# Decode layer on one core: the K part of pair 31 ahead of the output projection, the last O_l built on POOL, the residual joined in PSUM, the last rows of W_down in two transfers

## Chip, cores, metric

One core of a Trainium2 chip runs the whole kernel. The metric is the device time of one execution in microseconds (us). Times within a profile count from the start of its span. The device time is 1.2 to 1.4 us longer than the span of the profile in most runs.

PE is the matmul engine; DVE, ACT and POOL are the vector, scalar and GpSimd engines; SP issues most of the DMA transfers. SBUF is the on-chip memory that the engines read, PSUM the one that PE writes its products to. A transfer is spread over up to 16 DMA engines and has landed when the last of them has raised its semaphore. The granted clock is the share of full speed that the profile records for PE. Scatter means highest less lowest time.

## The reference, cut to what matters

```python
B, Sq, D = 2, 1, 512
Hq, Hkv, Sk, Dh = 32, 32, 8192, 128
F = 1376
h  = x + Attention(layernorm(x), k_cache, v_cache, wq, wo)      # 32 heads, 8192 cached positions
h2 = h + (relu(ln(h) @ W_gate) * (ln(h) @ W_up)) @ W_down       # W_down has 1376 rows = 10 * 128 + 96
```

K and V caches are 268 MB in bf16, and everything is read once. A "pair" is two heads of one batch row; there are 32, numbered 0 to 31, each with 4 MB of K and 4 MB of V.

## The kernel before: the parts that matter

Each engine has its own program, joined by semaphores. For one pair, DVE multiplies K by q for 96 of the 128 positions that each partition holds (one operation of 6.56 us, line 540), folds the product in four adds (line 549) and reduces it; PE transposes and multiplies the other 32 (`k_part`) and does P·V (`pv`). The last two pairs, P0 = 30 and P1 = 31, stand outside the loop. There, the heads done so far must pass through the output projection. For that, the scaled head output `O_cur` is spread into `O_l`, PE gathers it (`o_gather`), ACT copies it to `O_all`, and PE multiplies it with `X` (the rows of wo).

```python
def o_spread(g, prog, *t_oc):                 # five small operations; e is DVE or POOL
    e = prog.eng
    prog.wait(tok("og", g), *t_oc)
    ... prog.run(e.memset(O_l[...], 0.0)); prog.last()
    for a in range(2):
        e.tensor_copy(out=rsel[:, a, :], in_=rows[...])
        i = e.tensor_tensor(out=O_l[:, a, :, p0:p0 + n], in0=O_cur[...], in1=mask[...], op=ALU.mult)
    i.then_inc(l2p, 1)

# PE, after the loop (cut)
k_part(tail, P0, (2, 3, 4, 5), ((k2p, 1),))
nc.tensor.wait_ge(l2p, 1)
o_gather(tail)
...                                           # projection with X, 30 matmuls; then W product from os_sb
k_part(tail, P1, (10, 11, 12, 13), ((k2p, 2),))
pv(tail, P0, ...)
pv(tail, P1, ...)

# DVE, pair 30 (cut); the multiply of pair 31 comes behind it
normalize(Ob, dve.run, dve.last)
o_spread(g - 1, dve, dve.run(o_scale()))

# SP: the FFN weights; then at the very end of the stream
nc.sync.dma_start(wd_last[:], B_W_down[F - FR:]).then_inc(sem_wd[3], 16)      # FR = 96 rows

# end (cut): h is transposed to Tp[0], copied to h_r by DVE; W_down products go to Op[0]; then
t = dve.run(nc.vector.scalar_tensor_tensor(
    out=o_r, in0=Op[0][:, 0:128], scalar=r2[:, 0:1], in1=h_r, op0=ALU.mult, op1=ALU.add))
```

The softmax here doesn't subtract the row's maximum and nothing guards it: scores larger than these inputs give would overflow.

## Time and profile before

The kernel before took 660.57 us (median of 6 runs, 660.14 to 660.69).

| what | value | view |
|---|---|---|
| data moved, mean rate | 281 MB, 427 GB/s | page, slices |
| DMA queue's share of 16 engines' span | 99.3% | page, queues |
| P·V of pair 31 ends on PE | 648.0 us | chain of waits |
| last W_down rows: landed / multiplied | 656.06 / 656.38 us | landing semaphore / timeline |

The chain of waits on the page says what bounds the kernel:

```profile
DMA 76%; DVE 19%; PE 4%; issue 1%; ACT 1%; SPq 0%; DVEq 0%
```

Nearly all of it is loads. The DVE share is mostly the multiply that frees a K buffer for the next load. The last DMA issues, from the view of DMA issues (size, us from issue to landing):

```profile
slot<-in_B_W_up_dram SPq DMA_DIRECT2D x1, 1376.0 KB, 23.2
slot<-in_B_W_gate_dram SPq DMA_DIRECT2D x1, 1376.0 KB, 26.2
...
slot<-in_B_W_down_dram SPq DMA_DIRECT2D x1, 256.0 KB, 28.1
wd_last<-in_B_W_down_dram SPq DMA_DIRECT2D x1, 96.0 KB, 27.8
```

They were issued between 625.95 and 628.22 us, so the last rows land at 628.22 + 27.8 = 656.0. Time to landing is mostly queueing behind other transfers. PE's timeline (start, length, line, operation; in brackets the idle time before it and who ended it):

```profile
628.16 0.29 PE L431 MATMUL O<-rsel,O_l 128*128 128x30 bf16 x4 [0.80 <-DVE O_l L526]
628.78 3.58 PE L463 MATMUL O<-X,O_all 128*2 128x512 bf16 x30 [0.33 <-ACT O_all L671]
633.05 2.03 PE L469 MATMUL W<-sel,os_sb 128*128 128x2 f32 x8 [0.69 <-ACT os_sb L677]
634.94 1.95 PE L381 MATMUL T<-ident_f,slot 128*128 128x128 f32 x8
...
641.05 6.08 PE L405 MATMUL O<-slot,e 128*16 128x512 bf16 x56
...
647.38 0.61 PE L405 MATMUL O<-slot,e 128*16 128x512 bf16 x8
...
656.38 0.32 PE L808 MATMUL O<-wd_last,hd 96*2 96x128 bf16 x4
```

And the end of the chain of waits:

```profile
641.12 6.01 PE O L405 x54
...
648.04 0.61 ACT os_sb L569
...
655.13 0.19 DVE hd L789
...
655.36 1.37 PE O L808 x23
...
656.85 0.35 DVE kT L815
```

From 628 us on, the chain runs through PE and not through DMA, but the last rows had landed only 0.32 us before PE came to them. PE and DMA arrive almost together. One more reading bears on the change, the engines' timeline near pair 29 and 30 (POOL's copy of q_c, alone and beside a DVE add):

```profile
592.90 0.30 POOL L537 COPY q_c<-q_all 128x136 bf16<-128x136 bf16 x1
...
604.05 6.73 DVE L549 TENSOR_TENSOR prod<-prod 128x6144 bf16<-128x6144 bf16 x4
604.09 3.48 POOL L537 COPY q_c<-q_all 128x136 bf16<-128x136 bf16 x1 [10.89 <-DVEq L591]
```

The same copy takes 0.30 us alone and 3.48 us when it starts 0.04 us after the first of the four adds (which takes 3.36 us). The trace has 15 such pairs, with 3.40 to 3.48 us.

### The profile page before, as it was taken

What the parts mean: (1) busy time and instruction counts of PE and PEld (TensorE: products, weight loads), DVE (VectorE), ACT (ScalarE), POOL (GpSimd) and SP (SyncE); (2) the same over time, 40 slices, a digit from 0 to 9 for tenths busy, and PEclk for the clock granted to TensorE, in tenths of its full rate; (3) what the DMA queues carried; (4) which work ended last, traced back from release to release, by engine and by line L of the source; (5) the groups of instructions that cost most, each with busy time, mean ns of one, the idle gap of its engine ahead of it and who ended that gap; (6) DMA issues with size and microseconds to landing.
All of it is one profiled execution on the core that took longest, in us unless ns stands there. A gap on an engine that the chain in (4) does not pass through costs nothing.

```text
span 659.2 us, 7582 instructions
## 1 busy us (share of the span) xinstructions
PE 324.3 (49%) x3073; PEld 188.6 (29%) x3073; DVE 469.2 (71%) x280; ACT 213.6 (32%) x431; POOL 73.5 (11%) x125
## 2 busy tenths in 40 slices
PE   2753454435455343655535364443556444354577
PEld 0331332213233121433313142221324222133344
DVE  1585576788767678776768877676886767787991
ACT  1622333143342223334223343422324332333250
POOL 3002002020200202020020201002020110202000
PEclk9856556565756657555665756756555765655656
DMA  8999999999999999999999999999999999999997
GB/s 366 444 437 431 420 445 416 443 428 431 438 422 441 422 439 433 428 435 424 441 422 439 433 428 433 426 441 422 439 434 426 435 424 441 424 437 433 428 417 295
DMA packets 10653, 281.17 MB, mean 427 GB/s; under 512 B 1202, under 2 KB 1300, under 8 KB 1812
## 3 DMA queue, kind: packets, MB, share of 16 engines
q1 hardware_dynamic: 10632, 281.06, 99.3%
q8 instruction: 5, 0.08, 0.1%
q14 instruction: 4, 0.03, 0.0%
q10 hardware_dynamic: 12, 0.00, 0.0%
HBM read 281.05 MB, written 0.00 MB: 426 GB/s over the span
## 4 chain that ended last, share of the span: by engine, by line
DMA 76%; DVE 19%; PE 4%; issue 1%; ACT 1%; SPq 0%; DVEq 0%
DMA slot<-in_A_k_cache_dram 76%; DVE prod L540 16%; DVE prod L549 2%; PE O L405 1%; PE O L463 1%; PE T L381 0%; ACT kT L566 0%; PE W L469 0%; DVE scores L554 0%; PE S L756 0%; PE O L756 0%; PE O L808 0%; PE Ob L417 0%; SPq L172 0%; PE S L364 0%
## 5 line engine op out<-in xcount | busy, mean ns | idle before, releaser
L540 DVE TENSOR_TENSOR prod<-slot,q_c 128x12288 bf16<-128x12288 bf16 x32 | 209.9, 6558 | 148.0 <-DMA slot<-in_A_k_cache_dram 141.3
L405 PE MATMUL O<-slot,e 128*16 128x512 bf16 x1024 | 119.3, 621 | 219.9 <-ACT e L495 146.2
L549 DVE TENSOR_TENSOR prod<-prod 128x6144 bf16<-128x6144 bf16 (+3 forms) x128 | 212.2, 1657 | 7.8
L566 ACT ACTIVATE kT<-T 128x1024 bf16<-128x1024 bf16 x128 | 126.1, 1022 | 144.6 <-PE T L381 141.9
L381 PE MATMUL T<-ident_f,slot 128*128 128x128 f32 x512 | 108.6, 365 | 29.1 <-DVEq L587 29.1
L405 PEld LDWEIGHTS O<-slot,e 128*16 128x16 bf16 x1024 | 26.4, 114 | 287.0 <-ACT e L495 172.9
L495 ACT ACTIVATE e<-scores 64x96 bf16<-64x96 f32 x64 | 19.5, 304 | 239.6 <-DVEq L601 238.9
L381 PEld LDWEIGHTS T<-ident_f,slot 128*128 128x128 f32 x512 | 79.0, 188 | 44.2 <-DVEq L587 43.3
L537 POOL COPY q_c<-q_all 128x136 bf16<-128x136 bf16 x32 | 57.2, 1788 | 195.5 <-DVEq L591 152.5
L364 PE MATMUL S<-q_c,kT 128*128 128x4 bf16 x1024 | 47.4, 168 | 40.8 <-ACT kT L566 40.0
L364 PEld LDWEIGHTS S<-q_c,kT 128*128 128x128 bf16 x1024 | 39.1, 104 | 67.9 <-ACT kT L566 66.8
L417 PE MATMUL Ob<-sel,os_sb 128*128 128x4 f32 x136 | 30.1, 345 | 24.2 <-ACT os_sb L569 24.2
L417 PEld LDWEIGHTS Ob<-sel,os_sb 128*128 128x128 f32 x136 | 28.6, 311 | 26.1 <-ACT os_sb L569 26.1
L520 POOL MEMSET O_l<- 128x40 bf16 (+1 forms) x13 | 1.8, 136 | 303.9 <-DVEq L598 303.9
L554 DVE TENSOR_REDUCE scores<-prod 128x96 f32<-128x768 bf16 x32 | 30.5, 953 | 2.8
L566 ACT ACT_TABLE_LOAD x15 | 19.2, 1283 | 0.3
L495 ACT ACTIVATE e<-S 64x32 bf16<-64x32 f32 x64 | 13.0, 202 | 15.1 <-PE S L364 14.7
L569 ACT ACTIVATE os_sb<-O 128x512 f32<-128x512 f32 x17 | 10.1, 597 | 12.8 <-PE O L405 12.4
L495 ACT ACTIVATION_READ_ACCUMULATOR e<-S 64x1 f32 x64 | 12.8, 201 | 0.7
L495 ACT ACTIVATION_READ_ACCUMULATOR e<-scores 64x1 f32 x64 | 11.8, 185 | 0.0
L426 PEld LDWEIGHTS Ob<-zs,ones_f 128*128 128x128 f32 x30 | 7.1, 296 | 12.5 <-issue 12.5
L525 POOL COPY rsel<-rows 128x30 bf16<-128x30 bf16 x28 | 5.9, 209 | 33.3 <-DVEq L598 32.5
(104 smaller groups left out, 90.6 us busy)
## 6 DMA issues: line engine op xcount, KB each, us to landing
slot<-in_A_k_cache_dram SPq DMA_DIRECT2D x32, 4096.0 KB, 32.1
slot<-in_A_v_cache_dram SPq DMA_DIRECT2D x31, 4096.0 KB, 30.3
slot<-in_A_wq_dram SPq DMA_DIRECT2D x1, 4096.0 KB, 12.2
X<-in_A_wo_dram SPq DMA_DIRECT2D x1, 3840.0 KB, 45.8
slot<-in_A_v_cache_dram SPq DMA_DIRECT2D x1, 3072.0 KB, 23.3
slot<-in_B_W_up_dram SPq DMA_DIRECT2D x1, 1376.0 KB, 23.2
slot<-in_B_W_gate_dram SPq DMA_DIRECT2D x1, 1376.0 KB, 26.2
slot<-in_A_v_cache_dram SPq DMA_DIRECT2D x1, 1024.0 KB, 25.4
```

The lines of the kernel that those rows point to most:

```text
L364: i = nc.tensor.matmul(Sp[p % 2][:, 2 * jj:2 * jj + 4], lhsT=kv_[:, k, r, :], rhs=q_c[p % 2][:, 4 * r:4 * r + 4], start=(r == 0), stop=(r ...
L381: i = nc.tensor.transpose(Tp[g % 2][:, k * 128:(k + 1) * 128], k_t[:, j:j + 2, :].rearrange("p j d -> p (j d)").bitcast(F32), ident_f[:])
L405: i = nc.tensor.matmul(Op[0][c:c + 16, :], lhsT=e_t[q][:, j // VJ, :], rhs=v_t[:, j:j + VJ, :].rearrange("p j d -> p (j d)"), start=(q == ...
L417: i = nc.tensor.matmul(Ob[:, 0:4], lhsT=os_sb[:, jj * Dh:(jj + 1) * Dh], rhs=sel[:, 4 * jj:4 * jj + 4], start=(jj == 0), stop=(jj == VJ - 1))
L426: return nc.tensor.matmul(bank[:, ZC:ZC + 8], lhsT=ones_f[:], rhs=zs[:], start=True, stop=True)
L495: i = nc.scalar.activation(out=e_t[q][h, j0 // VJ:j1 // VJ, 8 * q:8 * q + 8].rearrange("p g (j a) -> p g j a", a=2)[:, :, :, a], in_=src(h ...
L537: nc.gpsimd.tensor_copy(out=q_c[p % 2][:], in_=q_all[:, p]).then_inc(g2d, 1)
L540: return nc.vector.tensor_tensor(out=prod[:, 0:JC, :], in0=tile((2 * p) % 4)[:, 0:JC, :], in1=q_c[p % 2][:, 8:QW].unsqueeze(1).broadcast_t ...
L549: run(nc.vector.tensor_tensor(out=prod[:, 0:JC, 0:w], in0=prod[:, 0:JC, 0:w], in1=prod[:, 0:JC, w:2 * w], op=ALU.add))
L554: return nc.vector.tensor_reduce(out=scores[p % PG][:, 0:JC], in_=prod[:, 0:JC, 0:8], axis=AX.X, op=ALU.add)
L566: to_pe(nc.scalar.activation(out=kT[gg % 2][:], in_=Tp[gg % 2][:].bitcast(BF16), func=ACT.Copy))
L569: to_pe(nc.scalar.activation(out=os_sb[:], in_=Op[0][:], func=ACT.Copy))
```

## The change

Intent: PE should not stand still for O_l, O_all and os_sb. The K part of pair 31 moves ahead of the gather and fills that time. DVE hands the five O_l operations to POOL and starts its last multiply sooner. The residual h goes into the same PSUM bank as the W_down products, so a copy of h and an add leave DVE. The last 96 rows of W_down are split 68 + 28.

```diff
                 k_part(tail, P0, (2, 3, 4, 5), ((k2p, 1),))
+                k_part(tail, P1, (7, 8, 9, 10), ((k2p, 2),))
                 nc.tensor.wait_ge(l2p, 1)
                 o_gather(tail)
   ... (projection)
+                pv(tail, P0, ((JC, J, ((slot_sem[1], 16),)), (0, JC, ((a2p, 13),))))
   ... (W product)
-                k_part(tail, P1, (10, 11, 12, 13), ((k2p, 2),))
-                pv(tail, P0, ((JC, J, ((slot_sem[1], 16), (a2p, 6))), (0, JC, ((a2p, 8),))))

-                            o_spread(g - 1, dve, dve.run(o_scale()))
+                            t_oc = dve.run(o_scale())
+                        if p == P0:
+                            o_spread(g - 1, pool, t_oc)

+    WD_TAIL = ((0, 68), (68, 28))
-                        nc.sync.dma_start(wd_last[:], B_W_down[F - FR:]).then_inc(sem_wd[3], 16)
+                        for k, (r0, n) in enumerate(WD_TAIL):
+                            nc.sync.dma_start(
+                                wd_last[r0:r0 + n], B_W_down[F - FR + r0:F - FR + r0 + n]).then_inc(sem_wd[3 + k], 16)

   # residual: hb is transposed into Op[0] with start=(c == 0), stop=False; u_sb is scaled by 1/var (r2);
   # the W_down products accumulate onto it; the variance products move ahead of the gate products
-                t = dve.run(nc.vector.scalar_tensor_tensor(
-                    out=o_r, in0=Op[0][:, 0:128], scalar=r2[:, 0:1], in1=h_r, op0=ALU.mult, op1=ALU.add))
+                t = dve.run(nc.vector.tensor_copy(out=o_r, in_=Op[0][:, 0:128]))
```

(ACT's order follows: the copies of pair 31's K come before O_all and os_sb.)

More of the change, by code (lines that the diff above doesn't have):

```diff
@@ L98, in bass_sequential_preLN__gqa_block_cached__glu_gated_reglu__decode_kernel @@
         sem_w = [S(f"w{i}") for i in range(2)]
-        sem_wd = [S(f"wd{i}") for i in range(4)]
+        sem_wd = [S(f"wd{i}") for i in range(5)]
         slot = [sb(f"slot{i}", [128, SLOT], BF16) for i in range(4)]
@@ L141, in bass_sequential_preLN__gqa_block_cached__glu_gated_reglu__decode_kernel @@
         vr = sb("vr", [128, B], F32)
-        ve = sb("ve", [128, 1], F32)
-        r2 = sb("r2", [128, 1], F32)
-        h_r = kT[0][:].bitcast(F32)[:, 0:128]
+        ve = sb("ve", [128, B], F32)
+        r2 = sb("r2", [128, B], F32)
         o_r = kT[1][:, 0:128]
@@ L457, in program @@
                 k_part(tail, P0, (2, 3, 4, 5), ((k2p, 1),))
+                k_part(tail, P1, (7, 8, 9, 10), ((k2p, 2),))
                 nc.tensor.wait_ge(l2p, 1)
                 o_gather(tail)
-                nc.tensor.wait_ge(a2p, 7)
+                nc.tensor.wait_ge(a2p, 12)
                 nc.tensor.wait_ge(sem_wo, 16)
@@ L466, in program @@
                 tail.mark("op", i)
-                nc.tensor.wait_ge(a2p, 9)
+                pv(tail, P0, ((JC, J, ((slot_sem[1], 16),)), (0, JC, ((a2p, 13),))))
+                nc.tensor.wait_ge(a2p, 14)
                 for c in range(DC):
@@ L669, in program @@
                         evacs()
+                    elif p == P1:
+                        evacs()
                         act.wait(tok("og", NI))
@@ L673, in program @@
                             in_=Op[1][:, 0:B * DR].rearrange("p (b r) -> p b r", r=DR), func=ACT.Copy))
-                        act.wait(t_s[p])
-                        exp_dve(p)
+                        act.wait(t_s[P0])
+                        exp_dve(P0)
                         act.wait(tok("op", NI))
                         to_pe(nc.scalar.activation(out=os_sb[:], in_=Op[1][:], func=ACT.Copy))
-                    elif p == P1:
-                        evacs()
                         act.wait(t_s[p])
@@ L766, in program @@
                     for c in range(DC):
-                        i = nc.tensor.matmul(
-                            Tp[0][32 * k:32 * k + B, c:128:DC], lhsT=hb[:, c * B:(c + 1) * B],
-                            rhs=ident[:, 32 * k:32 * k + 32], start=True, stop=True)
-                t_hr = pe.run(i)
-                pe.wait((sem_w[1], 16))
-                t_g = ffn_in(Op[1], wgt, 0, FC)
+                        nc.tensor.matmul(
+                            Op[0][32 * k:32 * k + B, c:128:DC], lhsT=hb[:, c * B:(c + 1) * B],
+                            rhs=ident[:, 32 * k:32 * k + 32], start=(c == 0), stop=False, skip_group_check=True)
                 dve.last()
@@ L782, in program @@
                 t_vh = dve.run(nc.vector.tensor_tensor(out=vh[:, B:], in0=vr[:], in1=vh[:, 0:B], op=ALU.subtract))
+                pe.wait(t_vh)
+                for k in range(2):
+                    i = nc.tensor.matmul(Sp[0][:, 32:32 + B], lhsT=onesn[:], rhs=vh[:, k * B:(k + 1) * B],
+                                         start=(k == 0), stop=(k == 1))
+                t_var = pe.run(i)
+                pe.wait((sem_w[1], 16))
+                t_g = ffn_in(Op[1], wgt, 0, FC)
+                dve.wait(t_var)
+                dve.run(nc.vector.tensor_scalar_add(out=ve[:], in0=Sp[0][:, 32:32 + B], scalar1=eps))
+                dve.last()
+                dve.run(nc.vector.reciprocal(out=r2[:], in_=ve[:]))
+                dve.last()
                 dve.wait(t_u)
-                dve.run(nc.vector.tensor_copy(out=u_sb[:], in_=Sp[1][:, 0:FC * B]))
-                dve.wait(t_hr)
-                dve.run(nc.vector.tensor_copy(out=h_r, in_=Tp[0][:, 0:128]))
+                dve.run(nc.vector.tensor_tensor(
+                    out=u_sb[:].rearrange("p (f b) -> p f b", b=B),
+                    in0=Sp[1][:, 0:FC * B].rearrange("p (f b) -> p f b", b=B),
+                    in1=r2[:].unsqueeze(1).broadcast_to([128, FC, B]), op=ALU.mult))
                 dve.last()
@@ L791, in program @@
                     in1=u_sb[:], op0=ALU.max, op1=ALU.mult))
-                pe.wait(t_vh)
-                for m in range(4):
-                    for k in range(2):
-                        i = nc.tensor.matmul(Sp[0][32 * m:32 * m + B, 32:33], lhsT=vh[:, k * B:(k + 1) * B],
-                                             rhs=onesn[:, 0:1], start=(k == 0), stop=(k == 1))
-                t_var = pe.run(i)
-                dve.wait(t_var)
-                dve.run(nc.vector.tensor_scalar_add(out=ve[:], in0=Sp[0][:, 32:33], scalar1=eps))
-                dve.last()
-                dve.run(nc.vector.reciprocal(out=r2[:], in_=ve[:]))
                 pe.wait(t_hd)
@@ L804, in program @@
                 for n, (f, k) in enumerate(order):
-                    pe.wait((sem_wd[k], 16))
+                    pe.wait((sem_wd[k], 16), (sem_wd[max(k, 2 * k - 2)], 16))
                     kp = 128 if f < 10 else FR
@@ L810, in program @@
                             rhs=(wdn[:, f, :] if f < 10 else wd_last[:])[:, 128 * m:128 * m + 128],
-                            start=(n == 0), stop=(n == FC - 1))
+                            start=False, stop=(n == FC - 1), skip_group_check=True)
                 t_y = pe.run(i)
-                dve.last()
                 dve.wait(t_y)
-                t = dve.run(nc.vector.scalar_tensor_tensor(
-                    out=o_r, in0=Op[0][:, 0:128], scalar=r2[:, 0:1], in1=h_r, op0=ALU.mult, op1=ALU.add))
+                t = dve.run(nc.vector.tensor_copy(out=o_r, in_=Op[0][:, 0:128]))
                 sp.wait(t)
```

## The prediction

> **What bounds the kernel now.** DMA. The page gives 281 MB at 427 GB/s with q1 busy 99.3% of 16 engines' span, and the chain of waits puts 76% on K loads. The change touches only the tail (from about 626 us), where two things run neck and neck. (1) DMA: issue plus time to landing puts W_up at 649.2, W_gate 652.5, W_down 654.2, 654.7, 655.8, the last 96 rows at 656.0. (2) PE (timeline, chain): O gather 628.16, projection 628.78 (3.6 us), os_sb 0.61, W product 2.03, K part of pair 31 634.9 to 641.1, P·V 641.05 to 648.0, then combination, FFN, W_down 655.36 to 656.7, DVE 0.35, output DMA about 2 us, end 659.2. So PE reaches the last W_down rows at 656.38, only 0.35 us after they landed. However much PE gains, the end cannot move forward by more than about 0.3 us.
>
> **Intent and cost.** DVE's five small O_l operations (627.57 to 628.1) go to POOL; pair 31's multiply starts about 0.5 us earlier, at 627.5; PE starts pair 31's K at about 627.6 and ends about 633.8, instead of idling for O_l, O_all and os_sb. If O_l were ready by then, projection, P·V(30), W product and P·V(31) would end near 647.0 instead of 648.0. Residual in PSUM: the 0.29 us copy of h leaves DVE, the closing 0.35 us becomes a copy of about 0.3; the variance products (0.2) move before the gate products. Net nearly 0. Last rows: 96 rows in one go use 16 engines. The Trainium skill ("DMA: Bandwidth & Descriptors", section "Why a DMA increments its semaphore by 16 and not by 1") takes the largest k up to 16 that divides the rows: 68 gives 4 engines, 28 gives 14, so late engines carry fewer rows. Landings of one transfer are spread by about 1.9 us; worth perhaps 0.1 to 0.2 us.
>
> **What I expect to go wrong.** POOL's O_l operations now run beside DVE's 6.56 us multiply and the adds. In this trace POOL's 0.30 us q_c copy takes 3.48 us whenever it starts just after an add: it ends 0.16 us after that add ends. The skill ("SBUF — State Buffer", "Who interferes with whom") says a DVE instruction with two SBUF inputs blocks a GpSimd instruction that reads SBUF; the trace agrees. The memset passes; the first rsel copy waits for the multiply (634.1). If one POOL operation slips through between DVE instructions, O_l is ready only after the third add, at 640.4; if two, at 637.6; if all, 634.4. At 640.4 PE idles from 633.8, then projection, P·V and W product follow in one burst of 12.8 us at half clock. Such a burst in the trace gains full clock after 3.4 to 6.8 us (clock 1.00 at 646.9 to 650.4), so it ends near 650.0, 2 us later than now; a warmer FFN gives back up to 0.8. That is +1 to +2.5 us. Two per gap: about 647.5, end set by DMA, -0.3.
>
> **Prediction.** 661.2 us, 8 in 10 within 659.9 to 664.0. Faster by over 2%: 0.005; within 2%: 0.985; slower: 0.01.
>
> **What would show it.** POOL's rsel copies lasting microseconds, each ending 0.1 to 0.2 us after a DVE multiply or add; PE idle before the O gather, released by POOL's O_l; P·V(31) ending after 648; the last wd_last landing no longer near the first W_down wait. If right on the other branch: O gather by 637, PE waiting for DMA at the last W_down products, end 0.2 to 0.4 us earlier.
>
> **What would make it wrong.** POOL's small operations slipping through together; DVE losing the port to POOL; the clock not rising (up to +6 us); the 4-engine transfer of 68 rows landing late.

## The result, and the profile after

The changed kernel took 660.48 us (median of 6 runs, 659.93 to 662.19) against 660.57 for the kernel before in the same rounds. The ratio is 1.0003 with a 95% interval of 0.999 to 1.0015: the same. (A ratio is the mean time of one kernel's fast runs over that of the other's fast runs of the same rounds, so it is not quite the ratio of the medians quoted.) The scatter is another matter: 2.3 us against 0.6.

POOL's timeline of the changed kernel:

```profile
627.77 0.15 POOL L520 MEMSET O_l<- 128x44 bf16 x1 [19.98 <-DVE O_cur L510]
627.99 6.38 POOL L525 COPY rsel<-rows 128x30 bf16<-128x30 bf16 x1
634.33 0.21 POOL L526 TENSOR_TENSOR O_l<-O_cur,mask 128x12 bf16<-128x12 bf16 x1
634.48 3.33 POOL L525 COPY rsel<-rows 128x30 bf16<-128x30 bf16 x1
637.77 0.21 POOL L526 TENSOR_TENSOR O_l<-O_cur,mask 128x10 bf16<-128x10 bf16 x1
```

And DVE's, beside it (the second line holds all four adds):

```profile
627.75 6.56 DVE L540 TENSOR_TENSOR prod<-slot,q_c 128x12288 bf16<-128x12288 bf16 x1
634.34 6.83 DVE L549 TENSOR_TENSOR prod<-prod 128x6144 bf16<-128x6144 bf16 x4
```

DVE's multiply ran from 627.75 to 634.30 and its first add from 634.34 to 637.74. The first copy, a 0.21 us operation elsewhere, waited out the multiply. The product behind it went through at once; the second copy waited out the add; the second product went through at once. So the operations went in pairs, and O_l was ready at 637.98. The memset, which reads nothing from SBUF, was not held. PE's timeline:

```profile
638.03 0.29 PE L431 MATMUL O<-rsel,O_l 128*128 128x30 bf16 x4 [4.16 <-POOL O_l L526]
638.65 3.15 PE L464 MATMUL O<-X,O_all 128*2 128x512 bf16 x30 [0.33 <-ACT O_all L675]
641.42 2.10 PE L405 MATMUL O<-slot,e 128*16 128x512 bf16 x32
...
647.13 0.61 PE L405 MATMUL O<-slot,e 128*16 128x512 bf16 x8
...
655.14 1.28 PE L812 MATMUL O<-slot,hd 128*2 128x128 bf16 x40 [0.36 <-DVE hd L803]
656.84 0.27 PE L812 MATMUL O<-wd_last,hd 96*2 96x128 bf16 x4 [0.42 <-DMA wd_last<-in_B_W_down_dram]
```

PE idled 4.16 us for O_l, yet P·V of pair 31 still ended 0.25 us earlier than before. The K part had been done ahead, and in this execution the granted clock was 1.00 from 641.2 to 651.5 us (before: 0.50 until 646.9). The last line shows the new end: PE is ready and waits for the last rows. The end of the chain of waits:

```profile
630.02 26.68 DMA wd_last<-in_B_W_down_dram
656.70 0.14 issue
656.84 0.31 PE O L812 x3
657.14 0.02 issue
657.17 0.29 DVE kT L818
```

Before, the end of the chain was PE; now it is the transfer of 28 rows. It landed at 656.70, which is 0.71 us after the third W_down block; the single transfer of before landed 0.20 us after that block.

### The profile page after: what moved, and what is told of

Its sections match the earlier page's. It is cut to its first block, busy times and chain, and to the rows that moved or that the text cites. A ratio compares the mean times of both kernels' runs of the same rounds, so it can differ in the third digit from the quotient of the medians.

```text
span 659.4 us, 7568 instructions
## 1 busy us (share of the span) xinstructions
PE 324.6 (49%) x3066; PEld 191.1 (29%) x3067; DVE 468.8 (71%) x274; ACT 214.1 (32%) x431; POOL 83.8 (13%) x130
## 4 chain that ended last, share of the span: by engine, by line
DMA 80%; DVE 15%; PE 3%; SPq 1%; issue 1%; ACT 0%; DVEq 0%
DMA slot<-in_A_k_cache_dram 69%; DVE prod L540 15%; DMA slot<-in_A_v_cache_dram 5%; DMA wd_last<-in_B_W_down_dram 4%; DMA slot<-in_A_wq_dram 2%; PE O L312 1%; PE O L405 1%; PE O L257 1%; PE T L381 0%; PE T L325 0%; SPq L709 0%; SPq L705 0%; PE Ob L417 0%; ACT kT L566 0%; SPq L701 0%
## 5 line engine op out<-in xcount | busy, mean ns | idle before, releaser
L405 PE MATMUL O<-slot,e 128*16 128x512 bf16 x1024 | 117.1, 608 | 218.4 <-ACT e L495 146.3
L381 PE MATMUL T<-ident_f,slot 128*128 128x128 f32 x512 | 113.1, 377 | 29.0 <-DVEq L587 29.0
L381 PEld LDWEIGHTS T<-ident_f,slot 128*128 128x128 f32 x512 | 81.8, 193 | 44.1 <-DVEq L587 44.1
L525 POOL COPY rsel<-rows 128x30 bf16<-128x30 bf16 x30 | 15.6, 519 | 33.4 <-DVEq L598 32.5
```

Source lines behind the costliest of these rows:

```text
L381: i = nc.tensor.transpose(Tp[g % 2][:, k * 128:(k + 1) * 128], k_t[:, j:j + 2, :].rearrange("p j d -> p (j d)").bitcast(F32), ident_f[:])
L405: i = nc.tensor.matmul(Op[0][c:c + 16, :], lhsT=e_t[q][:, j // VJ, :], rhs=v_t[:, j:j + VJ, :].rearrange("p j d -> p (j d)"), start=(q == ...
L525: e.tensor_copy(out=rsel[:, a, :], in_=rows[:, DR - off:2 * DR - off])
```

## The experiments

All are edits of one of the two kernels and give the right result. Two theories were set against each other. Theory D: DMA sets the end, and the split lands later and eats PE's gain. Theory P: POOL eats the gain, because O_l comes late.

Three sets ran, each on one chip with its own runs of the kernel before:

| set | label | runs | mean us | lowest to highest | before, mean | difference |
|---|---|---|---|---|---|---|
| – | changed, first rounds | 6 | 660.67 | 659.93 to 662.19 | 660.50 | +0.17 |
| 1 | after_again | 6 | 661.10 | 659.93 to 662.94 | 660.45 | +0.65 |
| 1 | after_one | 5 | 660.46 | 660.08 to 660.99 | 660.45 | +0.01 |
| 1 | before_split | 5 | 660.56 | 660.46 to 660.72 | 660.45 | +0.11 |
| 1 | after_one_dve | 5 | 660.14 | 660.00 to 660.37 | 660.45 | -0.31 |
| 2 | early_one | 5 | 660.24 | 660.05 to 660.57 | 660.38 | -0.15 |
| 2 | after_dve | 5 | 660.41 | 660.20 to 660.69 | 660.38 | +0.03 |
| 2 | one_dve_delay | 5 | 660.18 | 660.07 to 660.24 | 660.38 | -0.20 |
| 2 | before_delay | 5 | 660.71 | 660.38 to 660.94 | 660.38 | +0.33 |
| 3 | before_pool | 4 | 668.82 | 668.28 to 669.42 | 660.45 | +8.37 |
| 3 | half_one | 4 | 660.78 | 660.20 to 661.33 | 660.45 | +0.33 |
| 3 | before_resid | 5 | 660.20 | 660.03 to 660.49 | 660.45 | -0.25 |
| 3 | kahead | 5 | 660.26 | 660.17 to 660.40 | 660.45 | -0.20 |

Only before_pool is clear of noise by the interval of its ratio (1.0129, 1.0114 to 1.0145). For all others that interval is about plus or minus 0.13%, or 0.9 us, and holds 1. From the spread of the single runs alone, 0.15 to 0.3 us on a difference would be a fair 95% margin for the narrow ones. For after_again it would be 0.9, for half_one 0.5. So the order of the small differences leans on the traces more than on these numbers.

### The changed kernel once more

> The changed kernel unedited, as the control on this chip. Theory D (the end is set by the landing of the last W_down rows; the split into 68 and 28 rows lands 0.4 to 0.6 us later than one transfer and eats what the tensor engine gained): 660.2 to 660.7, equal to the kernel before within 0.3, with the tensor engine waiting 0.3 to 0.7 us for wd_last. Rival P (the gain was eaten on POOL: O_l late, so PE arrives no earlier): the same time, but the wait for wd_last would be an accident of this run and absent in this profile.

The mean was 661.10, above the 660.2 to 660.7 of both theories, and the profile is of another kind. PE's timeline:

```profile
641.50 3.44 PE L405 MATMUL O<-slot,e 128*16 128x512 bf16 x32
644.86 2.03 PE L471 MATMUL W<-sel,os_sb 128*128 128x2 f32 x8
...
648.54 0.61 PE L405 MATMUL O<-slot,e 128*16 128x512 bf16 x8
...
657.59 0.32 PE L812 MATMUL O<-wd_last,hd 96*2 96x128 bf16 x4
```

O_l came at the same moment (637.9), but P·V of pair 30 took 3.44 us instead of 2.10. The clock records show why: 1.00 was granted only from 644.2 us, 3.0 us later than in the first profile. P·V of pair 31 ended at 649.15 instead of 647.74, and PE never waited for W_down, which had landed at 656.12. In this execution PE set the end and POOL's delay was on the chain. So neither theory holds in every run. After O_l arrives, PE has one burst of ten us to do, and how fast it goes depends on when the clock rises. Of the twelve runs of the changed kernel, eight have spans of 658.7 to 659.4 us and four of 660.1 to 660.3. This last profile is one of the four (660.2), the first one of the eight (659.4). (Two of the four, 662.19 and 662.94, also have 2.1 and 2.6 us outside the span instead of 1.2; that part is not explained.) The Trainium skill ("TensorE: Matmul & The Clock Gate", "What's actually happening") says that the gate opens after a busy window of about 3.4 us, and that this window is free-running and does not start with the kernel. The clock records agree with a free-running window: in all traces kept here, every complete stretch at one clock lasts 3.41 us or a multiple of it, and in the two profiles the rise came 3.0 us apart for the same instructions at the same places. That a whole window must be busy does not come out of them: in the loop of the kernel before, the clock rose 2.6 to 4.9 us after PE began to work again (166.49 and 169.07 us in the shortest case, after an idle time of 5.38 us).

### One transfer, or two, for the last rows

```diff
-    WD_TAIL = ((0, 68), (68, 28))          # after_one: the changed kernel with
+    WD_TAIL = ((0, FR),)
```

> The changed kernel with the last 96 rows in one transfer again, all else as changed (POOL still builds O_l late). Theory D: the last landing moves back to 0.2 us after that of the third W_down block, PE waits at most 0.2 us for it, and the time is 0.3 to 0.6 us lower than the changed kernel, 0.2 to 0.4 lower than the kernel before. Rival P: no change against the changed kernel (within 0.1), since PE arrives as late as before.

The mean was 660.46: lower than the control of its set by 0.6 (which the control's scatter of 3.0 us leaves unclear), but equal to the kernel before, not 0.2 to 0.4 below. Its profile has PE at the last rows at 656.56, right behind their landing at 656.52: neither waits for the other. With O_l late, removing the split is not enough.

`before_split` is the opposite: the kernel before with only the `WD_TAIL` loop.

> The kernel before with only the split of the last rows into 68 and 28. Theory D: the last landing is 0.6 to 0.8 us after that of the third W_down block instead of 0.2, PE waits for it, and the time is 0.2 to 0.4 us above the kernel before. If the split does what it was meant for (fewer rows on the late DMA engines): 0 to 0.2 us lower. Rival P: within 0.1 of the kernel before.

The mean was 660.56, 0.11 above the kernel before, less than theory D asked for, and nowhere the gain that the split was made for. In its profile the last rows landed 0.40 us after the third block.

### O_l on DVE again

```diff
-                            t_oc = dve.run(o_scale())     # after_one_dve: one transfer, and
+                            o_spread(g - 1, dve, dve.run(o_scale()))
-                        if p == P0:
-                            o_spread(g - 1, pool, t_oc)
```

> One transfer for the last rows, and DVE builds O_l before its multiply as in the kernel before, so PE finds it ready at the end of the K part of pair 31. Theory D: PE's P.V of pair 31 ends 0.5 to 1 us earlier than in the changed kernel, but then waits for W_gate and W_down, so the time equals that of the changed kernel with one transfer within 0.1. Rival P: lower by another 0.5 to 1 us.

The mean was 660.14, the lowest of all and below both kernels, with a scatter of 0.4 us. PE's waits for V and for W_gate:

```profile
646.18 0.61 PE L405 MATMUL O<-slot,e 128*16 128x512 bf16 x8 [0.79 <-DMA slot<-in_A_v_cache_dram]
...
652.75 1.72 PE L758 MATMUL O<-d_b,slot 128*128 128x2 bf16 x44 [0.47 <-DMA slot<-in_B_W_gate_dram]
```

The end of its chain of waits:

```profile
628.04 24.66 DMA slot<-in_B_W_gate_dram
...
652.75 1.74 PE O L758 x44
...
656.00 0.54 PE O L810 x12
...
656.57 0.29 DVE kT L816
```

P·V of pair 31 waited 0.79 us for the last part of V, the gate products 0.47 us for W_gate, and the last W_down products for their blocks (landed 655.96 and 656.20). PE is early everywhere and everything ends on DMA. Against after_one this is 0.3 lower, not "within 0.1" as theory D said. With five runs each the margin on that difference is about 0.4, so that taking the work from POOL pays is likely but not shown by the times; the traces show the end of P·V of pair 31 1.35 us earlier (646.79 against 648.14).

`after_dve` is the same with the split kept:

> Changed kernel with O_l on DVE, the split of the last rows kept. PE is early here, so the split shows by itself against the run with one transfer (660.08). If the split costs (theory D): 0.1 to 0.5 us slower than that, 660.2 to 660.6, PE waiting up to 0.7 us for wd_last. If it gains: 0.1 to 0.2 us faster, 659.9.

Here PE is early and the split shows by itself:

```profile
656.66 0.28 PE L810 MATMUL O<-wd_last,hd 96*2 96x128 bf16 x4 [0.37 <-DMA wd_last<-in_B_W_down_dram]
```

The rows landed at 656.52, 0.65 us after the third block. Against its own rounds of the kernel before the version stands at +0.03, and without the split at -0.31 (another chip; the margin on the difference of the two is about 0.3). In all, four traces with the split have the last rows 0.71, 0.21, 0.40 and 0.65 us behind the third block; ten traces with one transfer have 0.20 to 0.25. So counted from the third block, the split landed later in three traces and level in one, and never gained.

### Does PE or DMA set the end?

Two dummy DVE copies were put ahead of `hd`, on PE's path to W_down, in both kinds of kernel:

```diff
+                for _ in range(2):
+                    dve.run(nc.vector.tensor_copy(out=d2[:], in_=d_b[:])); dve.last()
                 t_hd = dve.run(nc.vector.scalar_tensor_tensor(
```

> The version with O_l on DVE and one transfer, plus two dummy DVE copies (about 0.2 us each, 0.4 together) on the path to the first W_down product. If DMA sets the end there: at most 0.1 us slower than without (660.1 to 660.2), since PE's wait for W_down shrinks instead. If PE sets it: 0.4 slower, 660.5.

> The kernel before with the same two dummy copies. Its profile shows PE at the last W_down rows 0.3 us after they landed, so PE sets the end in that run: 0.3 to 0.4 us slower than the kernel before, 660.7 to 660.9. If DMA set its end in most runs: under 0.15 slower.

The two copies took 0.38 us in both traces. On the version with O_l on DVE the difference to before went from -0.31 to -0.20: the wait for W_down took up most of the delay, and the first W_down product began at 655.32 instead of 654.82 without moving the last ones (656.34). On the kernel before, the mean rose by 0.33. So the end of the kernel before is set by PE, at least in most runs, that of the version with O_l on DVE by DMA, and the room between them is about 0.3 us. (The first figure compares two sets, and both have margins of 0.2 to 0.3 us. Nor is PE last in every execution of a kernel with the old order: see before_resid below.)

### POOL by itself

`before_pool` changes one thing in the kernel before, who builds O_l, and leaves the gather where it was:

> The kernel before with one thing changed: POOL instead of DVE builds the last O_l; the projection still stands ahead of the K part of pair 31, so nothing hides O_l. Theory P: O_l is ready only after the first add, near 637.7, so O gather starts near 637.9 instead of 628.2 and everything behind it moves by 9.7 us less what a warmer clock gives back (up to 2 us): 668 to 670.5 us. If POOL were only as slow as its own five operations (about 0.9 us): 661.

```profile
638.09 0.29 PE L431 MATMUL O<-rsel,O_l 128*128 128x30 bf16 x4 [8.91 <-POOL O_l L526]
```

The gather started at 638.09 and the mean rose by 8.37 us. Moving some 0.5 us of small work (627.57 to 628.11 on DVE) from DVE to POOL left PE idle for 8.91 us before the gather instead of 0.80, because that work then waited behind DVE. In the changed kernel the K part of pair 31 hides about half of this (4.16 us of idle time are left).

`early_one` keeps the work on POOL but does what does not need O_cur (memset, both rsel copies) before the wait for it, and uses one transfer for the last rows:

```diff
+    pool.wait(tok("og", g - 1))
+    ... memset of O_l, both rsel copies; pool.last()
     pool.wait(t_oc)
     ... the two multiplies
```

> Changed kernel, one transfer for the last rows, and POOL does its memset and both rsel copies of the last O_l before it waits for O_cur, in its idle time from 607 us on; only the two multiplies stay behind DVE. Theory P (POOL's reads wait out DVE's two-input operations; two pass per gap): both multiplies pass in the one gap after DVE's 6.56 us multiply, O gather starts at 634.5 to 635 instead of 638, P.V of pair 31 ends 1 to 2 us before that of the changed kernel, and the time is 660.0 to 660.3 with a scatter under 0.5 us, as with O_l on DVE. If POOL is slow for another reason (its own dispatch, or the semaphore), O gather stays at 636 or later and the scatter of the changed kernel, 659.9 to 662.9, stays.

POOL's and then PE's timeline:

```profile
607.56 0.15 POOL L657 MEMSET O_l<- 128x44 bf16 x1
607.63 1.83 POOL L660 COPY rsel<-rows 128x30 bf16<-128x30 bf16 x2
627.71 6.68 POOL L666 TENSOR_TENSOR O_l<-O_cur,mask 128x12 bf16<-128x12 bf16 x2 [18.25 <-DVE O_cur L510]
```

```profile
634.84 0.27 PE L431 MATMUL O<-rsel,O_l 128*128 128x30 bf16 x4
```

Both multiplies were through 0.24 us after DVE's multiply had ended (634.16), and PE came to the gather without any wait. The mean was 660.24 and the scatter 0.5 us. Nothing of POOL's speed was changed, only which of its reads stand behind DVE. That settles where the late O_l came from.

`half_one` leaves multiply, copy, multiply behind DVE, to see how many operations pass per gap:

> As the version with POOL's preparation done early, but only the memset and the first rsel copy are early; multiply, copy, multiply stay behind DVE. If two POOL reads pass per gap between DVE's two-input operations: multiply and copy pass after DVE's 6.56 us multiply, the last waits for the first add, O gather starts at 637.7 to 638.3 as in the changed kernel, time 660.2 to 661. If three or more can pass: O gather at 634.6 to 635.2, time 660.1.

```profile
627.75 6.52 POOL L667 TENSOR_TENSOR O_l<-O_cur,mask 128x12 bf16<-128x12 bf16 x1 [18.37 <-DVE O_cur L510]
634.21 0.20 POOL L666 COPY rsel<-rows 128x30 bf16<-128x30 bf16 x1
634.37 3.32 POOL L667 TENSOR_TENSOR O_l<-O_cur,mask 128x10 bf16<-128x10 bf16 x1
```

Two passed and the third waited for the add (gather at 637.75). The mean was 660.78 and the scatter 1.1 us: a late O_l again comes with a wider scatter. (Only its fastest run, 660.20, was profiled, so that the clock makes this scatter is not shown.)

### The other two parts alone

> The kernel before with only the residual joined in PSUM (and the variance in front of the gate products). Both theories: little of it lies on the path: one DVE copy of 0.29 us is taken away beside the gate products, the closing operation 0.35 becomes 0.29 us, the variance products add under 0.1 us before the gate: 660.2 to 660.5, within 0.15 of the kernel before.

The residual in PSUM alone gave 660.20, 0.25 under the kernel before, more than expected. Its trace shows 0.06 us of it (the closing operation is 0.29 instead of 0.35 us). The rest is within the margin (0.2 us) and need not come from the edit: in its profile the clock rose at 644.95 us, 2.0 us earlier than in that of the kernel before, P·V of pair 31 ended at 647.12, and PE waited for W_gate (0.26 us) and W_down (0.20 us). In before_split's profile, too, it rose early (643.62) and PE waited 0.60 us for W_gate. So with the old order as well, which of the two comes last can change with the clock.

> The kernel before with only the K part of pair 31 put ahead of the projection (O_l on DVE, residual and last rows as before). Theory: PE reaches V and the FFN weights before they land, as in the version with O_l on DVE and one transfer, and the end is set by the last landing: 660.0 to 660.3, scatter under 0.5 us; 0 to 0.1 above that version, for the closing operation.

The K part ahead alone, with O_l on DVE, gave 660.26 with a scatter of 0.23 us. Its gather started right behind the K part (634.99), and PE waited 0.42 us for W_gate. This one move holds about 0.2 of the 0.3 us that there are to gain in the tail.

## Why the prediction was right or wrong

- **The time.** Right: 660.48 lies within 659.9 to 664.0 and the call "within 2%" holds. The centre, 661.2, was 0.7 above the first median; the mean of all twelve runs of the changed kernel is 660.88. That the time fell inside is in part luck: the range also holds 660.57, the time of no change at all, and its centre came from the branch with one POOL operation per gap, which did not happen. The branch that did happen was given as 0.3 us below the kernel before; measured were 0.17 and 0.65 above it in the two sets.
- **"However much PE gains, the end cannot move forward by more than about 0.3 us."** Right. The best version is 0.31 below, with PE waiting for DMA in three places, and a delay of 0.38 us on it costs 0.11 (measured in another set).
- **POOL held by DVE's two-input operations.** Right, as the Trainium skill ("SBUF — State Buffer", "Who interferes with whom") has it: reads were held (6.38 and 3.33 us), the memset was not, and before_pool shows the cost bare.
- **"If one POOL operation slips through between DVE instructions, O_l is ready only after the third add, at 640.4."** This was the branch that I leaned on, and it failed. Two pass per gap, in after, after_again, before_pool and half_one alike, so O_l was ready at 637.98. The branch "Two per gap: about 647.5" named P·V's end well for the first profile (647.74), but not for the second (649.15).
- **The clock.** The sum carried one end of the burst, 650.0. The burst did reach full clock, but 3.0 us apart in the two profiles, and P·V of pair 31 ended at 647.74 and 649.15. This fits the scatter of the changed kernel (four runs of twelve about one us longer), but one execution of each kind was profiled; that the clock makes all four is not shown.
- **"end set by DMA, -0.3", with the split "worth perhaps 0.1 to 0.2 us".** The sign of the split was wrong. The reason given holds as far as it goes: the landing semaphores show 4 engines at work for 68 rows and 14 for 28, as the skill's rule for k, cited in the prediction, says. But one of those four engines was late in each of four traces: of the four landings of the 68 rows, the last came 0.48 to 0.82 us after the third. That engine had 17 rows of this transfer to carry where it had 6 before. The term is a loss of about 0.3 us where PE is early (+0.03 against -0.31, on two chips). That the 17 rows on a late engine cause it is read from the landings and was not tested by itself.
- **The sum.** PE gains about 1.3 us if O_l is ready (P·V of pair 31 ends at 646.67 in early_one's profile, at 648.0 before), of which 0.3 can show. Late O_l takes this away in part (647.74) or, with a late clock, more than wholly (649.15); the split takes about 0.3 where PE is early. What is left is a difference that can't be told from zero, and a wider scatter.

## What to carry to other kernels

Moving small operations from DVE to POOL freed little time here (0.54 us on DVE) and cost much: where they read SBUF while DVE streamed two-input operations, each pair of them waited for a whole DVE instruction. So do all of it that has its inputs early before that stream begins. Where two chains end within a few tenths of a microsecond of each other, speeding up one is worth only that difference; find it first by delaying the chain on purpose. A short burst of matmuls after an idle PE ran at a clock that differed between two executions, so look at the scatter and at more than one profile before explaining a median.

## What the Trainium skill lacked or had wrong

- "SBUF — State Buffer", "SBUF: two separate sides": it says that the loser of the shared port is held for the whole instruction, which these runs confirm (6.38 us behind a multiply of 6.56). Neither it nor "Who interferes with whom" says that two short GpSimd reads pass in one gap between dependent DVE operations (the gap is 0.035 us in the trace), nor what that costs DVE: the add behind them took 3.41 us instead of 3.36.
- "DMA: Bandwidth & Descriptors", "Latency and other measured facts": it names slow engines 7 and 15 and puts them down, as a best guess, to rings that these queues do not use. In the kernel before, the engines of one transfer landed within 0.5 us of each other for the first three, and 1.7 to 1.9 us apart from 34.5 us on, just behind an instruction packet of 16 KB that took 1.06 us at 32.4 us. The number of engines that landed over 0.6 us behind the first of their transfer went from 0 to 1, 2, 3 and 4, each step behind such a packet (16 KB at 32.4 and 56.2 us, 8 KB at 181.0 and 489.7 us). The lateness stayed to the end. No page says that instruction fetches delay data transfers. It is a coincidence of times, seen in the traces of both kernels, and was not tested; if it is the cause, the instruction fetch is what spreads the last landing by 1.9 us.
- "TensorE: Matmul & The Clock Gate", "What's actually happening": the free-running window is there and agrees. The page puts the variation of the rise at plus or minus 0.5 us (and says further on that the number of slow matmuls differs from run to run, without a figure in time); here the rise came 3.0 us apart in two profiles of one kernel, whose spans differ by 0.8 us.
